# Reading P, q and k as rounded float32 in the TensorE transposes of a fused attention and gated-convolution kernel, with q and k in chunks of 128 and a work order planned by repeated passes

## The chip, the cores and the metric

The kernel runs on one core of one Trainium2 chip. The metric is the device time of one execution in microseconds (us). The kernel before takes 806.61 us, the median of three runs that lie between 805.94 and 806.62.

## The reference, cut to what matters

Eight batches, eight heads, 576 tokens, 64 values per head. Attention is causal by blocks of 64 tokens; its output, with the heads side by side, goes through a two-layer block with a three-tap convolution as a gate:

```python
scores = scale * np.matmul(q, k.transpose(0, 1, 3, 2))           # q, k, v: 8 x 8 x 576 x 64
scores = np.where(block_i >= block_j, scores, -1000000000.0)      # blocks of 64 tokens
scores = scores - np.max(scores, axis=-1, keepdims=True)
attn = np.exp(scores)
attn = attn / (np.sum(attn, axis=-1, keepdims=True) + 1e-09)
x = np.matmul(attn, v)                                            # -> 8 x 576 x 512
h = np.maximum(x @ w_in, 0.0)                                     # 512 -> 1024
conv_out[t] = sum(conv_w[k] * h[t + k - 1] for k in range(3))     # zero outside the sequence
out = (h / (1.0 + np.exp(-conv_out))) @ w_out                     # 1024 -> 512
```

## The kernel before, in words

**Numbers.** Nearly every product is made from operands that are split in two: a "high" part rounded to the format `float32r` (rounded float32; `F32R` in the code, `fp32r` or plain `f32` in the profile) and a "low" rest, also `float32r`. A product is then three TensorE passes: high by high, high by low, low by high. The names end in `h` and `l` (`qh`, `ql`, `ptbh`, `ptbl`, `xh`, `xl`, `wih`, `wil`, `woh`, `wol`, `gh`, `gl`).

**Tiling.** Heads go in pairs, 32 of them, four to a batch; a pair fills the 128 partitions with two times 64 values. The four pairs of the first batch are worked in two visits each ("A", the first 256 tokens, and "B", the rest), so that their part of the second stage can begin while weights are still loading; the other 28 pairs are one visit each.

For a pair of the 28:

- `load_nat` (L398) loads q and k with tokens on partitions into `qn` and `kn`: 6 pieces of 96 tokens, one DMA per head and tensor, from SyncE's queue (SP).
- `stage_t` (L707) turns them: for each of q and k two groups of three transposes (L725, 96x128 to 128x96) into one PSUM bank of the tag `w`, then ScalarE (ACT, L729) copies the high part and VectorE (DVE, L732) makes the low part, 288 tokens at a time. A transpose is a TensorE instruction in which the data are the stationary operand, loaded as weights, and the identity matrix `ident` is the moving one. DMAs from SP's queue then move high and low halves to other partitions (`qa`, `qb`, `ka`, `kb`, `qz`, `qdl`, L742 to L762).
- `stage_s` (L908) makes the scores of four blocks of 128 queries (L930, L932), their row maximum (DVE, L940) and the exponential P with its sum (ACT, L943), in tiles `p0` to `p3` of 128 to 512 keys. `last_s` (L872) does the last 64 queries of both heads together, in `p4` (576 keys). GpSimd (POOL) multiplies each P by the reciprocal of its sum (L859).
- `stage_x` (L1100) turns P: `one_bank` transposes 1 to 4 blocks of 128x128 into a bank of the tag `w` (L1116; 25 of them per pair), and ACT (L1126) and DVE (L1129) split the result into `ptah`/`ptal` or `ptbh`/`ptbl`.
- `stage_pv` (L1175) multiplies with v (L1203, L1207).

When four pairs of a batch are done, `ffn` runs the second stage in two halves of 288 tokens: the first layer (L1283), the gate on ACT, DVE and POOL, the second layer (L1342), the store. Its matmuls are small pieces of work that the order spreads among the attention of the next batch.

**The order.** Nothing is issued in the order of the code. Every piece of work is recorded by `Plan.op` with its engine, an assumed duration, the pieces that it depends on, the buffers that it uses and a target time. `Plan.order` (L97) then plays the program once on five assumed engines: each engine takes, of the pieces that are ready, the one with the lowest target. Second-stage matmuls are "paced": they may run at most `WINDOW` us ahead of the earliest attention piece that is still waiting. Where TensorE would idle for more than 0.4 us, `order` puts fill matmuls in (L1473), which compute nothing that is used. The result is one fixed order per engine. For a transpose group the plan assumes 0.109 us per P transpose and 0.084 us per q or k transpose.

Of the kernel before, what the change touches and what calls it, by code (L numbers as in the profile page):

```python
# [23 lines left out]
class Buf:  # L24


    def __init__(self, pool, shape, dtype, tag):
        self.args = (pool, shape, dtype, tag)
        self.uses = []
        self.before = []  # L30
        self.t = None

    @property
    def ap(self):
        if self.t is None:
            pool, shape, dtype, tag = self.args
            self.t = pool.tile(shape, dtype, tag=tag, name=tag)
        return self.t


# [13 lines left out]
class Plan:  # L54
# [41 lines left out]

    def order(self, window, skip, fill, clock):  # L97
        work, tags, unit, least, spare = fill
# [23 lines left out]
        for o in self.ops:  # L122
            o.left = len(o.deps)
            for d in o.deps:
                d.outs.append(o)
# [108 lines left out]
def kernel(  # L234
# [10 lines left out]
    nc = tc.nc  # L245
# [8 lines left out]
    HS = S // 2  # L254
    R = 6
    TP = S // R
    SCALE = 1.0 / 8.0
# [51 lines left out]
    WL0, WLS = -49.08, 2.41  # L309
    WINDOW = 19.66  # L310

    cp = ctx.enter_context(tc.tile_pool(name="cp", bufs=1))
# [14 lines left out]
    def one(shape, dtype, tag):  # L327
        return pl.buf(cp, shape, dtype, tag, 1)
# [26 lines left out]
    def two(shape, dtype, tag):  # L355
        return pl.buf(p2, shape, dtype, tag, 2)


    def c_mm(n, m=P):
        return max(n * 0.000447 + 0.005, 0.086 * m / P)  # L360

    def c_act(n, psum=True, ap=False, acc=False):
# [8 lines left out]
    def c_dma(n, packet):  # L371
        return n / (213e3 if packet < 512 else 290e3 if packet < 1024 else 330e3 if packet < 2048 else 390e3)
# [23 lines left out]


    def load_nat(p, at, part=None):  # L398
        b, h0 = p // NP, 2 * (p % NP)
        res = []  # L400
        for src, tag in ((q, "qn"), (k, "kn")):
            n = one([TP, R, 2, D], F32, tag)
            tok, w, r_ = (slice(Q1, S), 80, 4) if part else (slice(0, S), TP, R)

            def go(src=src, n=n, tok=tok, w=w, r_=r_):
                for j in range(2):
                    nc.sync.dma_start(out=n.ap[0:w, 0:r_, j, :],
                                      in_=src[b, h0 + j, tok, :].rearrange("(r p) d -> p r d", r=r_))

            res.append((n, pl.op(SP, 1.0, go, at, bufs=[n], xfer=2 * c_dma(r_ * w * D * 4, 256))))  # L410
        return res
# [295 lines left out]
    def stage_t(nat, at):  # L707
# [5 lines left out]
        for which, (n, ld) in enumerate(nat):  # L713
# [3 lines left out]
            es = []  # L717
            for j in range(2):
                tb = bank("tv")
                nn = HS  # L720
                tok = slice(HS * j, HS * j + HS)

                def tr(n=n, tb=tb, j=j):
                    for r in range(3):
                        nc.tensor.transpose(tb.ap[:, r * TP:(r + 1) * TP],  # L725
                                            n.ap[0:TP, 3 * j + r].rearrange("p j d -> p (j d)"), ident[0:TP, 0:TP])
# [74 lines left out]
    def rest_t(nat, at):  # L801
# [4 lines left out]
        for which, (n, ld) in enumerate(nat):  # L806
            hi, lo = (t["qa"], t["qb"]) if which == 0 else (t["kh"], t["kl"])
            scale = SCALE if which == 0 else 1.0
            w, rs, c0 = 80, ((0, 4),), Q1
            for j, (r0, r1) in enumerate(rs):  # L810
                tb = bank("tv")
                nn = w * (r1 - r0)
                tok = slice(c0 + w * r0, c0 + w * r1)

                def tr(n=n, tb=tb, r0=r0, r1=r1, w=w):
                    for r in range(r0, r1):
                        nc.tensor.transpose(tb.ap[:, (r - r0) * w:(r - r0 + 1) * w],
                                            n.ap[0:w, r].rearrange("p j d -> p (j d)"), ident[0:w, 0:w])
# [9 lines left out]
                o = pl.op(PE, (r1 - r0) * (w / 1200.0 + 0.004), tr, t0, deps=[ld], bufs=[n, tb], area=0.36)  # L828
# [43 lines left out]
    def last_s(t, ready4, t0, pb, done, exps, part):  # L872
        st4 = keep([P, 16], F32, "st4", 2, EPS)
        p4 = one([P, S], F32, "p4")
        pb[4] = p4
# [32 lines left out]
    def stage_s(ops, hh, at, part, shared):  # L908
# [52 lines left out]
    def stage_sb(ops, at):  # L961
# [4 lines left out]
        for z, i in enumerate((2, 3)):  # L966
# [18 lines left out]
            for hh in range(2):  # L985
                pt = two([P, nk], F32, f"p{i}")
                pb[hh][i] = pt
# [33 lines left out]
    def stage_sa(ops, at):  # L1021
# [3 lines left out]
        sb = [bank("s"), bank("f")]  # L1025
        pb = [{i: two([P, 128 * (i + 1)], F32, f"p{i}") for i in range(2)} for _ in range(2)]
        done, exps = [{}, {}], []
# [72 lines left out]
    def stage_x(pbd, hh, at, part, shared):  # L1100
# [10 lines left out]
        def one_bank(trs, rows, n, hi, lo, deps, t0, bufs_p, bufs_hi, bufs_lo, sub_ok, tag, shape):  # L1111
            tb = bank(tag)

            def tr():
                for z, (x, c, kk, col) in enumerate(trs):
                    nc.tensor.matmul(tb.ap[0:kk, col:col + P], pb[x].ap[:, 128 * c:128 * c + kk], ident,  # L1116
                                     start=(z == 0), stop=True, is_transpose=True, skip_group_check=True)

            o = pl.op(PE, len(trs) * 0.109 + 0.003, tr, t0, deps=deps, bufs=[tb] + bufs_p, area=0.49)

# [389 lines left out]
```

## Time and profile before

| what | value |
|---|---|
| runs | 806.61 us (805.94 to 806.62) |
| profiled execution, its own span from first to last instruction | 805.2 us |
| TensorE (PE) busy, 5381 matmuls | 793.4 us, 99% |
| VectorE (DVE) busy | 649.9 us, 81% |
| ScalarE (ACT) busy | 614.6 us, 76% |
| GpSimd (POOL) busy | 424.1 us, 53% |
| P transposes, L1116 | 800, of which 32 are 64 wide |
| q and k transposes of the 28 pairs, L725 | 336 |
| q and k transposes of visit "B", L817 | 32 |
| fill matmuls, L1473 | 100, all before 96 us |

The span is the only time that belongs to the profiled execution itself; the median of the runs is 1.4 us above it.

How to read the profile: a line such as `L1116 PE MATMUL w<-ident,p` is an operation of line 1116 on TensorE that writes a tile of the tag `w` from the moving operand `ident` and the stationary operand `p`. `PEld` is the load of the stationary operand, which can run beside the matmul before it. Matmuls are pipelined: the "mean" of one is how long it was in the engine, not how far apart two of them start. The distance from start to start is what TensorE spends on one; it is read from the timeline and from the chain of work.

### The profile page before, as it was taken

The page shows a single profiled execution, that of the slowest core. Times are in us where ns is not written, and L with a number is a line of the kernel's source. Part 1 is how long each engine was busy: PE and PEld are TensorE (multiplying, and loading weights), DVE is VectorE, ACT ScalarE, POOL GpSimd, SP SyncE. Part 2 cuts the span into 40 slices and gives each one's busy share as a digit, 9 for nine tenths or more (in the row PEclk, how much of TensorE's full clock was granted, in tenths as well). Part 3 has the DMA queues.
Part 4 walks back from the last instruction along what each step waited for, and adds up shares of the span by engine and source line. Part 5 has one row for each costly group of instructions (what it writes and reads, how often), then busy time and mean ns, then how long its engine had stood idle before and what let it go on. Part 6 is the DMA issues. An engine that isn't in the chain of part 4 may idle for free.

```text
span 805.2 us, 17261 instructions
## 1 busy us (share of the span) xinstructions
PE 793.4 (99%) x5381; PEld 712.1 (88%) x5381; DVE 649.9 (81%) x1889; ACT 614.6 (76%) x1769; POOL 424.1 (53%) x607
## 2 busy tenths in 40 slices
PE   8999999999999999999999999999999999999998
PEld 5668889888989899898989889898989989899996
DVE  6898989988979779797988869798887959887541
ACT  4769978977968769796978769697877858787652
POOL 3345556666655446565555645555455635546431
PEclk9999999999999999999999999999999999999999
DMA  9423556475445545444455544445554434540001
GB/s 231 143 65 92 144 122 149 111 182 145 104 116 125 134 118 120 110 101 120 120 135 135 122 117 99 102 115 135 135 122 118 110 98 105 136 105 14 14 27 40
DMA packets 163327, 91.35 MB, mean 113 GB/s; under 512 B 134540, under 2 KB 138660, under 8 KB 163236
## 3 DMA queue, kind: packets, MB, share of 16 engines
q1 hardware_dynamic: 162692, 90.12, 45.1%
q8 instruction: 44, 0.72, 0.4%
q14 instruction: 47, 0.39, 0.2%
q10 hardware_dynamic: 544, 0.13, 0.1%
HBM read 38.30 MB, written 9.44 MB: 59 GB/s over the span
## 4 chain that ended last, share of the span: by engine, by line
PE 82%; ACT 6%; DVE 5%; DMA 2%; issue 2%; POOL 2%; SPq 1%; ACTq 0%; POOLq 0%; DVEq 0%
PE f L1283 21%; PE f L1342 19%; PE w L1207 10%; PE w L1116 9%; PE s L930 4%; PE s L932 4%; PE w L1342 3%; PE s L885 3%; PE w L725 3%; PE s L1283 2%; ACT ptbh L1126 1%; DMA vn<-in_v_dram 1%; POOL vv L437 1%; DMA gh<-in_moe_w_in_dram 1%; PE s L1473 1%
## 5 line engine op out<-in xcount | busy, mean ns | idle before, releaser
L859 POOL TENSOR_SCALAR p<-p,st 128x256 f32<-128x256 f32 (+4 forms) x256 | 140.4, 562 | 139.0 <-DVE st L853 82.8
L1323 POOL TENSOR_TENSOR gl<-t,gh 128x288 fp32r<-128x288 f32 (+2 forms) x128 | 104.1, 816 | 148.8 <-ACT gh L1320 145.4
L943 ACT ACTIVATE p<-s,st 128x128 f32<-128x128 f32 x224 | 118.0, 527 | 41.9 <-DVE st L940 40.8
L1116 PE MATMUL w<-ident,p 128*128 128x128 f32 (+1 forms) x800 | 125.0, 274 | 0.7 <-DVE xl L1231 0.3
L940 DVE TENSOR_REDUCE st<-s 128x1 f32<-128x128 f32 x224 | 107.5, 484 | 3.4
L1126 ACT ACTIVATE ptbh<-w 128x384 fp32r<-128x384 f32 (+1 forms) x192 | 93.7, 508 | 21.7 <-PE w L1116 19.2
L1116 PEld LDWEIGHTS w<-ident,p 128*128 128x128 f32 (+1 forms) x800 | 95.0, 139 | 15.5 <-POOL p L859 1.7
L1342 PE MATMUL f<-woh,gh 128*128 128x512 f32 x248 | 103.9, 419 | 0.0
L1283 PE MATMUL f<-xh,wih 128*128 128x290 f32 (+2 forms) x480 | 97.7, 307 | 0.3 <-DVE t L1316 0.3
L1342 PE MATMUL f<-woh,gl 128*128 128x512 f32 x248 | 97.9, 395 | 0.0
L1129 DVE TENSOR_TENSOR ptbl<-w,ptbh 128x512 fp32r<-128x512 f32 (+1 forms) x144 | 89.6, 633 | 10.3 <-ACT ptbh L1126 7.4
L1342 PE MATMUL f<-wol,gh 128*128 128x512 f32 x248 | 97.7, 394 | 0.0
L1283 PE MATMUL f<-xh,wil 128*128 128x290 f32 (+2 forms) x480 | 94.5, 304 | 0.0
L1283 PE MATMUL f<-xl,wih 128*128 128x290 f32 (+2 forms) x480 | 93.3, 304 | 0.0
L1304 DVE SCALAR_TENSOR_TENSOR t<-f,cw,t 128x287 f32<-128x287 f32 (+3 forms) x120 | 59.9, 499 | 19.0 <-ACT t L1300 17.3
L1283 PEld LDWEIGHTS f<-xh,wih 128*128 128x128 f32 x480 | 73.1, 189 | 1.9 <-DVE t L1316 0.5
L1283 PEld LDWEIGHTS f<-xl,wih 128*128 128x128 f32 x480 | 72.9, 189 | 1.0
L1283 PEld LDWEIGHTS f<-xh,wil 128*128 128x128 f32 x480 | 73.2, 189 | 0.4
L932 PE MATMUL s<-kl,qz 128*128 128x128 f32 x224 | 72.1, 322 | 0.0
L1320 ACT ACTIVATE gh<-t 128x288 fp32r<-128x288 f32 (+2 forms) x128 | 56.7, 445 | 8.3 <-DVE t L1316 7.4
L1300 ACT ACTIVATE t<-f,cw 128x288 f32<-128x288 f32 (+2 forms) x120 | 59.9, 499 | 3.8
L1308 DVE SCALAR_TENSOR_TENSOR t<-f,cw,t 128x288 f32<-128x288 f32 (+3 forms) x120 | 60.6, 505 | 1.3
(230 smaller groups left out, 2001.0 us busy)
## 6 DMA issues: line engine op xcount, KB each, us to landing
out_dram<-stage SPq DMA_DIRECT2D x36, 256.0 KB, 2.2
vn<-in_v_dram SPq DMA_DIRECT2D x64, 128.0 KB, 2.9
qn<-in_q_dram SPq DMA_DIRECT2D x56, 144.0 KB, 2.9
kn<-in_k_dram SPq DMA_DIRECT2D x56, 144.0 KB, 3.1
ka<-kh SPq DMA_DIRECT2D x56, 144.0 KB, 2.6
kb<-kh SPq DMA_DIRECT2D x56, 144.0 KB, 2.6
qa<-qh SPq DMA_DIRECT2D x28, 144.0 KB, 2.4
qb<-qh SPq DMA_DIRECT2D x28, 144.0 KB, 2.6
```

The lines of the kernel that those rows point to most:

```text
L859: nc.gpsimd.tensor_scalar(out=pt.ap, in0=pt.ap, scalar1=st.ap[:, col:col + 1], scalar2=0.0, op0=ALU.mult, op1=ALU.add)
L932: nc.tensor.matmul(sb.ap[:, 0:nk], qz.ap[:, z:z + 128], kl.ap[:, 0:nk], start=False, stop=True)
L940: nc.vector.tensor_reduce(out=st.ap[:, i:i + 1], in_=sb.ap[:, 0:nk], op=ALU.max, axis=AX.X, negate=True)
L943: nc.scalar.activation(out=pt.ap[:, 0:nk], in_=sb.ap[:, 0:nk], func=AF.Exp, bias=st.ap[:, i:i + 1], accum_out=st.ap[:, 4 + 2 * i:5 + 2 * i])
L1116: nc.tensor.matmul(tb.ap[0:kk, col:col + P], pb[x].ap[:, 128 * c:128 * c + kk], ident, start=(z == 0), stop=True, is_transpose=True, skip_ ...
L1126: nc.scalar.activation(out=hi(), in_=src(), func=AF.Copy)
L1129: nc.vector.tensor_tensor(out=lo(), in0=src(), in1=hi(), op=ALU.subtract)
L1207: nc.tensor.matmul(tb.ap[0:m, q0 - qa:qb - qa], vv.ap[:, chunk(c), hh, w[ps_]], pm.ap[:, 128 * c + q0:128 * c + qb] if qa == 0 else pm.ap[ ...
L1283: nc.tensor.matmul(fb.ap[:, 0:n2], wt[:, c, fs], xs[c][xi].ap[:, x0:x0 + n2], start=(n + c - c0 == 0), stop=(n + c - c0 == 3 * NCC - 1))
L1308: nc.vector.scalar_tensor_tensor(out=t.ap[:, 0:i1], in0=fb.ap[:, own + 1:own + 1 + i1], scalar=cw[:, 2 * NFC + f:2 * NFC + f + 1], in1=t.a ...
L1323: nc.gpsimd.tensor_tensor(out=gbuf[1].ap[:, f, carry:carry + no], in0=t.ap[:, 0:no], in1=gbuf[0].ap[:, f, carry:carry + no], op=ALU.subtract)
L1342: nc.tensor.matmul(fb.ap[:, 0:DM], gbuf[a].ap[:, f, cs], w[:, f, :], start=(f == 0 and n == 0), stop=(f == NFC - 1 and n == 2))
```

## The change

1. **A second name for the same bytes.** The tiles `p0` to `p4`, `qn` and `kn` no longer come from tile pools. They lie at fixed addresses, each under two names: a float32 one, which ACT, POOL and the DMAs write, and a `float32r` one (`raw`, named `p3r`, `qnr` and so on), which only the transposes read. The numbers of buffers stay: two of each `p0` to `p3`, one of `p4`, `qn`, `kn`.
2. **All P, q and k transposes use `rident`**, the identity in `float32r`, and write PSUM through a `float32r` view. The transposes of the first 256 tokens of the first batch (L784) stay as they were.
3. **q and k in chunks of 128 tokens**: four chunks of 128 and one of 64 where there were six of 96 (in visit "B" two of 128 and one of 64 where there were four of 80). The two groups per tensor become three chunks (384 tokens) and two (192), where both were 288. Each load is three DMAs where it was two.
4. **The order by passes.** `order` now calls the forward play (`forward`, the old code) 25 times. After each, `late` plays the program backward from its end and gives every piece, as its new target, the latest time at which it could run; `WINDOW` is lifted after the first round. The order with the earliest planned end is kept.
5. **Assumed durations**: a group of n transposes counts as max(0.083 n - 0.035, 0.06) us.

```diff
+class Twin(Buf):
+    def __init__(self, pair):
+        self.t, self.raw = pair
...
+    def late(self, done):
...
+                if not left[d.seq]:
+                    heapq.heappush(future[d.eng], (rt[d.seq], top - d.end, d.seq, d))
+        return [top - r for r in res]
+
+    def order(self, window, skip, fill, clock, rounds):
+        best, least = None, 1e30
+        for _ in range(rounds + 1):
+            done = self.forward(window, skip, fill, clock)
+            end = max(o.end for o in self.ops)
+            if end < least:
+                best, least = done, end
+            for o, t in zip(self.ops, self.late(done)):
+                o.target = t
+            window = 1e9
+        return best
+
+    def forward(self, window, skip, fill, clock):
...
+    spans = [(f"p{i}", 128 * (i + 1), 2) for i in range(4)] + [("p4", S, 1), ("qn", 5 * P, 1), ("kn", 5 * P, 1)]
...
+            twins[tag].append([nc.alloc_sbuf_tensor_at(f"{tag}{x}{i}", [P, n], d, offset=at).ap()
+                               for x, d in (("f", F32), ("r", F32R))])
...
+    def c_tr(n):
+        return max(n * 0.083 - 0.035, 0.06)
...
+    def chunks(n, tb, cs):
+        for z, c in enumerate(cs):
+            m = P if c < 4 else 64
+            nc.tensor.transpose(tb.ap[:, P * z:P * z + m].bitcast(F32R), n.raw[0:m, P * c:P * c + P], rident[0:m, 0:m])
...
-            n = one([TP, R, 2, D], F32, tag)
+            n = twin(tag)
...
                 for j in range(2):
-                    nc.sync.dma_start(out=n.ap[0:w, 0:r_, j, :],
-                                      in_=src[b, h0 + j, tok, :].rearrange("(r p) d -> p r d", r=r_))
+                    nc.sync.dma_start(out=x[:, c0:4, j, :],
+                                      in_=src[b, h0 + j, P * c0:4 * P, :].rearrange("(c p) d -> p c d", p=P))
+                nc.sync.dma_start(out=x[0:64, 4, :, :], in_=src[b, h0:h0 + 2, 4 * P:S, :].rearrange("j p d -> p j d"))
...
-            for j in range(2):
+            for j, cs in enumerate(((0, 1, 2), (3, 4))):
                 tb = bank("tv")
-                nn = HS
-                tok = slice(HS * j, HS * j + HS)
+                nn = (384, 192)[j]
+                tok = slice(384 * j, 384 * j + nn)
...
-                o = pl.op(PE, 3 * (TP / 1200.0 + 0.004), tr, t0 + 0.5 * j, deps=[ld], bufs=[n, tb], area=0.36)
+                o = pl.op(PE, c_tr(len(cs)), tr, t0 + 0.5 * j, deps=[ld], bufs=[n, tb], area=0.7)
...
-            pt = two([P, nk], F32, f"p{i}")
+            pt = twin(f"p{i}")
...
-                    nc.tensor.matmul(tb.ap[0:kk, col:col + P], pb[x].ap[:, 128 * c:128 * c + kk], ident,
+                    nc.tensor.matmul(tb.ap[0:kk, col:col + P].bitcast(F32R), pb[x].raw[:, 128 * c:128 * c + kk], rident,
                                      start=(z == 0), stop=True, is_transpose=True, skip_group_check=True)
 
-            o = pl.op(PE, len(trs) * 0.109 + 0.003, tr, t0, deps=deps, bufs=[tb] + bufs_p, area=0.49)
+            o = pl.op(PE, c_tr(len(trs)), tr, t0, deps=deps, bufs=[tb] + bufs_p, area=0.8)
...
-    for o in pl.order(WINDOW, SKIP, (work, NBANK, 0.234, LEAST, SPARE), CLOCK):
+    for o in pl.order(WINDOW, SKIP, (work, NBANK, 0.234, LEAST, SPARE), CLOCK, ROUNDS):
```

The change moves work on every engine, because the plan is made anew. Two places are shown, on the two engines that the change touches itself. Rows are an engine's instructions in issue order; what is in brackets are the engines or DMA queues that an instruction waits for.

First TensorE, in the middle of the program, where the q and k transposes of the next pair stand among the scores and the second layer. Before (`kb`, `qb`, `kl`, `qz` are operands of the scores, `woh`, `gh` of the second layer, `p_` with a number is a P tile):

```order
L1342 MATMUL f<-woh,gl 128x512
L725 MATMUL w<-ident,qn 128x96 [waits PE_49]
L725 MATMUL w<-ident,qn 128x96 x2
L725 MATMUL w<-ident,qn 128x96 [waits DVE_49]
L725 MATMUL w<-ident,qn 128x96 x2
L930 MATMUL s<-kb,qb 128x256 [waits Activation_49]
L932 MATMUL s<-kl,qz_105 128x256
L1342 MATMUL f<-woh,gh 128x512
L1342 MATMUL f<-wol,gh 128x512
L1342 MATMUL f<-woh,gl 128x512
L725 MATMUL w<-ident,kn 128x96 [waits DMAHW7_49,DMAHW0_49,DVE_49]
L725 MATMUL w<-ident,kn 128x96 x2
```

The same place of the changed kernel (`qnr`, `knr` and `p0r` are the second names):

```order
L1024 MATMUL s<-kl,qz_127 128x256
L491 MATMUL w<-rident,qnr_95 128x128 [waits PE_49]
L491 MATMUL w<-rident,qnr_95 128x128 x2
L491 MATMUL w<-rident,qnr_95 128x128 [waits DVE_49]
L491 MATMUL w<-rident,qnr_95 128x64
L491 MATMUL w<-rident,knr_97 128x128 [waits DMAHW6_49,DMAHW7_49,DMAHW0_49,DVE_49]
L491 MATMUL w<-rident,knr_97 128x128 x2
L1022 MATMUL s<-kb,qb 128x384 [waits Activation_49]
L1024 MATMUL s<-kl,qz_127 128x384
```

Six transposes of q became five, the first group of k moved up to stand right behind them, ahead of a block of scores, and k now waits for three DMAs.

Then SyncE's queue at one pair, between two loads of k. Before:

```order
L407 DMA qn<-in_q_dram 96x6x64 x2
L762 DMA qa<-qh 64x576
L762 DMA qb<-qh 64x576
L742 DMA qz_105<-qh 64x576
L762 DMA qa<-ql 64x576
L762 DMA qb<-ql 64x576
L742 DMA qz_105<-qh 64x512
L762 DMA ka<-kh 64x576 x2
L762 DMA kb<-kh 64x576 x2
```

In the changed kernel:

```order
L503 DMA qnf_94<-in_q_dram 128x4x64 x2
L505 DMA qnf_94<-in_q_dram 64x2x64
L857 DMA qa<-qh 64x576
L837 DMA qz_127<-qh 64x576
L857 DMA qa<-ql 64x576
L837 DMA qz_127<-qh 64x512
L857 DMA ka<-kh 64x576 x2
L837 DMA qz_127<-qh 64x64
L846 DMA qdl_129<-ql 64x64 x2
L857 DMA qb<-qh 64x576
L857 DMA qb<-ql 64x576
L857 DMA kb<-kh 64x576 x2
```

The load of q is three issues ahead of the moves in place of two, and what the second head's scores need (`qb`, `kb`) now comes behind what the first head's need.

More of the change, by code (lines that the diff above doesn't have):

```diff
@@ L92, in op @@
         return o
-    def order(self, window, skip, fill, clock):
+    def late(self, done):
+        ops = self.ops
+        top = max(o.end for o in ops)
+        left = [len(o.outs) for o in ops]
+        rt = [0.0] * len(ops)
+        free, port = [0.0] * 5, 0.0
+        ready, future = [[] for _ in range(5)], [[] for _ in range(5)]
+        for o in ops:
+            if not left[o.seq]:
+                heapq.heappush(future[o.eng], (0.0, top - o.end, o.seq, o))
+        n = len(ops)
+        res = [0.0] * n
+        while n:
+            best = None
+            for e in range(5):
+                t = free[e]
+                while future[e] and future[e][0][0] <= t:
+                    o = heapq.heappop(future[e])[3]
+                    heapq.heappush(ready[e], (top - o.end, o.seq, o))
+                if ready[e]:
+                    p, _, o = ready[e][0]
+                    cand = (max(t, port) if o.port else t, p, e, o, 0)
+                elif future[e]:
+                    t, p, _, o = future[e][0]
+                    cand = (max(t, port) if o.port else t, p, e, o, 1)
+                else:
+                    continue
+                if best is None or cand[:2] < best[:2]:
+                    best = cand
+            t, _, e, o, where = best
+            heapq.heappop(future[e] if where else ready[e])
+            end = t + (o.end - o.start)
+            free[e] = end
+            if o.port:
+                port = end
+            res[o.seq] = end
+            n -= 1
+            for d in o.deps:
+                lat = self.DRAIN[d.eng] + (self.SIGNAL[e] if d.eng != e else 0.0) if (d.eng != PE or e != PE) else 0.0
+                rt[d.seq] = max(rt[d.seq], end + d.lat + lat)
+                left[d.seq] -= 1
+                if not left[d.seq]:
+                    heapq.heappush(future[d.eng], (rt[d.seq], top - d.end, d.seq, d))
+        return [top - r for r in res]
@@ L717, in stage_t, with tr @@
             es = []
[L718 removed]
+            for j, cs in enumerate(((0, 1, 2), (3, 4))):
                 tb = bank("tv")
[L720 to L726 removed]
+                nn = (384, 192)[j]
+                tok = slice(384 * j, 384 * j + nn)
+                def tr(n=n, tb=tb, cs=cs):
+                    chunks(n, tb, cs)
                 def ev_hi(tb=tb, hi=hi, scale=scale, tok=tok, nn=nn):
@@ L808, in rest_t, with tr @@
             scale = SCALE if which == 0 else 1.0
-            w, rs, c0 = 80, ((0, 4),), Q1
-            for j, (r0, r1) in enumerate(rs):
+            for j in range(1):
                 tb = bank("tv")
[L812 to L818, printed above, removed]
+                nn = S - Q1
+                tok = slice(Q1, S)
+                def tr(n=n, tb=tb):
+                    chunks(n, tb, (2, 3, 4))
                 def ev_hi(tb=tb, hi=hi, scale=scale, tok=tok, nn=nn):
```

37 lines of the change are left out of this document (28 added, 9 removed).

## The prediction, made before the changed kernel was run

> **What bounds the kernel now.** I read the page first, then busy time by stretch, then who waited for whom, then the chain of work in the middle, and last the timeline there. The page:
>
> ```profile
> span 805.2 us, 17261 instructions
> PE 793.4 (99%) x5381; PEld 712.1 (88%) x5381; DVE 649.9 (81%) x1889; ACT 614.6 (76%) x1769; POOL 424.1 (53%) x607
> PEclk9999999999999999999999999999999999999999
> PE f L1283 21%; PE f L1342 19%; PE w L1207 10%; PE w L1116 9%; PE s L930 4%; PE s L932 4%; PE w L1342 3%; PE s L885 3%; PE w L725 3%; PE s L1283 2%; ACT ptbh L1126 1%; DMA vn<-in_v_dram 1%; POOL vv L437 1%; DMA gh<-in_moe_w_in_dram 1%; PE s L1473 1%
> ```
>
> TensorE is busy 99% of the span at the full clock, and the chain that ended last runs over it, with 9% in the P transposes (L1116) and 3% in those of q and k (L725). A busy TensorE can still be a waiting one, so the stretches (us from:to, length, busy time and instructions of PE, PEld, DVE, ACT and POOL, clock, DMA share, GB/s) and TensorE's waits between 100 and 740 us come next:
>
> ```profile
> 80.00:100.00 20.00, 19.81 (x146) 16.15 (x145) 19.52 (x59) 19.32 (x53) 10.17 (x16) 1.00 0.54 148
> 100.00:740.00 640.00, 637.61 (x4419) 584.80 (x4420) 542.67 (x1602) 508.51 (x1484) 359.62 (x501) 1.00 0.49 119
> 740.00:801.00 61.00, 61.00 (x351) 54.33 (x350) 23.75 (x51) 29.50 (x73) 17.94 (x23) 1.00 0.07 27
> ...
> PE s L930 <- DMA ka<-kh: 1.1, 1, 1.1
> PE f L606 <- DVE wol L553: 0.4, 1, 0.4
> PE f L1283 <- DVE t L1316: 0.3, 1, 0.3
> PE s L930 <- ACT p L943: 0.2, 1, 0.2
> ```
>
> From 100 to 740 us TensorE waited 2.0 us in all, while DVE worked 542.67 of 640 us, 85%. From 740 us on there is only the second layer's stage of the last batch, and TensorE fills all of it. So TensorE's own work sets the end, and what is taken from it after 100 us should come off the span, as long as no other engine takes its place. Before 100 us this is not so: in the stretch from 80 to 100 us DVE was busy for 19.52 us of 20.
>
> **What a transpose costs.** Start-to-start distances come from the chain of work (start, duration, line, count), for P, for q, for the small ones of visit "B" and, last, for six ordinary matmuls of 512 columns:
>
> ```profile
> 406.80 0.77 PE w L1116 x7
> ...
> 424.47 0.50 PE w L725 x6
> ...
> 47.16 0.28 PE w L817 x4
> ...
> 408.70 1.40 PE f L1342 x6
> ```
>
> A P transpose takes 0.77/7 = 0.110 us, one of 96 columns 0.50/6 = 0.083, one of 80 columns 0.28/4 = 0.070, an ordinary matmul 1.40/6 = 0.233. The transposes scale with the columns of the moving identity, some 0.00086 us each, twice the 0.233/512 = 0.00046 of an ordinary matmul. All three load 128 columns of stationary data, so that load, read as float32 in a transpose, fits into 0.070 us.
>
> In rounded float32 the trace has only ordinary matmuls. From the timeline, two score matmuls of 128 columns between long ones; and the mean duration of weight loads of four kinds:
>
> ```profile
> 423.38 0.22 PE L930 MATMUL s<-kb,qb 128*128 128x128 f32 x1
> 423.44 0.27 PE L932 MATMUL s<-kl,qz 128*128 128x128 f32 x1
> 423.55 0.45 PE L1342 MATMUL f<-woh,gh 128*128 128x512 f32 x1
> ...
> L1116 PEld LDWEIGHTS w<-ident,p 128*128 128x128 f32 (+1 forms) x800 | 95.0, 139 | 15.5 <-POOL p L859 1.7 <-POOL p L1072 1.0 <-DVE ptbl L1129 0.8
> L725 PEld LDWEIGHTS w<-ident,qn 96*128 96x128 f32 x168 | 18.4, 140 | 2.4 <-issue 0.2
> L932 PEld LDWEIGHTS s<-kl,qz 128*128 128x128 f32 x224 | 42.5, 190 | 2.0
> L1207 PEld LDWEIGHTS w<-ptbl,vv 128*64 128x64 f32 x256 | 26.8, 136 | 0.9
> ```
>
> The second of the two starts 0.06 us after the first, because its weights were loaded under the long matmul before. The third starts 0.11 us after the second: its load could begin only with the second matmul, and 128 columns of rounded float32 need that long. A load of 64 columns is 54 ns shorter (190 - 136), which fits 0.11 us for 128. The float32 load in a transpose takes 139 ns for 128 columns, like an ordinary one of 64.
>
> So a rounded transpose of 128 columns moves in 0.06 us, and the question is its load. No row shows a rounded load in the transposing form. **Bounds** for the distance L between two transposes of a run: 0.058 (the move, 128 x 0.00046, if the load is as short as the float32 one) and 0.110 (if it is like every other rounded load). The nearest rows are the loads of the same 4-byte words in the same form, L1116 and L725; the shortest distance at which such a load of 128 columns has been seen to go by is the 0.070 of L817. I take L = 0.070.
>
> **The sum.** In the printed order the change has 1104 transposes in 317 unbroken runs: 800 of P, 304 of q and k. The last of a run is followed by an ordinary load, so it costs 0.11 whatever L is. Before there are 800 of P, 336 and 32 of q and k, in 316 runs, 97 of which end on q or k and pay 0.025 more there (0.108 - 0.083).
>
> - Before: 800 x 0.110 + 336 x 0.083 + 32 x 0.070 + 97 x 0.025 = 88.0 + 27.9 + 2.2 + 2.4 = 120.5 us.
> - After: 787 x L + 317 x 0.11 = 55.1 + 34.9 = 90.0 us at L = 0.070, a saving of 30.5. At 0.058 it is 40.0, at the 0.083 of today's q and k 20.3, at 0.110 it is -0.9.
>
> How many of them stand where TensorE is the bound, by the P transposes alone in the two stretches:
>
> ```profile
> 0.00:100.00 100.00, 13.29 (x81) 9.08 (x81) 1.00 0.51 135
> 100.00:740.00 640.00, 111.69 (x719) 85.97 (x719) 1.00 0.49 119
> ```
>
> - 719 of 800 come after 100 us, nine tenths: **-27.4** (from -36.0 at 0.058 to -18.3 at 0.083).
>
> In the Trainium skill, page "TensorE: Matmul & The Clock Gate", section "Back-to-back issue gap", a stream of load and matmul pairs of 128 columns settles at about 81 ns each. As an estimate by that figure the term would be -19.7 and the time some 788 us; the 0.070 of L817 went by with loads of the same 128 columns, so here the row goes ahead of the rule, which stays inside the range.
>
> Other edits, term by term:
>
> - *Fill matmuls* go from 100 to 90, and from 87 to 67 ahead of the first matmul of the second stage. Ten times 0.233 is 2.3 us of planned idleness less, all before 100 us. But the stretch 80 to 100 us shows DVE and ACT full, and what frees there need not come off: **-1**, between 0 and -2.3.
> - *Evictions.* ACT and DVE still copy twice per tensor, 384 + 192 tokens in place of 288 + 288: the same instructions and elements, nothing.
> - *Buffers.* As many as before, at fixed places: the same waits for a free one, nothing. If a stall hides here, it would show as TensorE or ACT waiting for a P tile; there is none above 0.2 us now.
> - *Loads.* One more DMA per tensor on SP's queue, ahead of the moves that the scores need. The queue at a pair (start, duration):
>
> ```profile
> 402.29 0.86 SPq L407 DMA_DIRECT2D qn<-in_q_dram  x2
> ...
> 405.85 0.55 SPq L762 DMA_DIRECT2D qa<-qh  x1
> 406.50 0.54 SPq L762 DMA_DIRECT2D qa<-ql  x1
> ...
> 414.18 1.08 SPq L407 DMA_DIRECT2D kn<-in_k_dram  x2
> 417.11 0.37 SPq L1355 DMA_DIRECT2D out_dram<-stage  x1
> ```
>
> An issue takes 0.86/2 = 0.43 us. The moves at this pair are issued from 405.85 to 414.18, and scores (L930) waited for one in only one place (1.1 us, above), so the cover is the second-stage matmuls that stand between q's transposes and the next scores: nothing now, 0.43 us per tensor if that cover went.
>
> *New waits.* With 27 us less, DVE's 542.67 us fall into 613 us, 89%, and every chain ACT - DVE - POOL has 4% less time under TensorE. The new order holds no fill after the first stage, so it leaves no planned gap of 0.4 us. But it is one order in fixed queues, and the row of 80 to 100 us shows that DVE can reach 98%. I put **+2**, between 0 and +7.
>
> 805.2 - 27.4 - 1 + 2 = 778.8 us of span, and 1.4 us more for the median of the runs (806.6 against a span of 805.2): **780.2 us**. The ends: 805.2 - 36.0 - 2.3 + 1.4 = 768.3 and 805.2 - 18.3 + 7 + 1.4 = 795.3.
>
> **The rivals.**
>
> *The load stays long.* If rounded weights load in a transpose as they do everywhere else in this trace, L is 0.110. P gains nothing, and five chunks of q cost more than six pieces of 96. That is -0.9 us of saving and a time of 805.2 + 0.9 + 1.4 = 807.5, no change. The same holds if the move of the rounded identity keeps the 0.00086 us per column of today. In its favour: every rounded load of 128 columns takes some 190 ns. Against: the load does depend on the form, since a transpose's takes 139 ns for the same 128 columns and 140 with 96 rows. Break-even is at (120.5 - 34.9)/787 = 0.109. Chance 0.09.
>
> The Trainium skill's rule for a load, in "LDWEIGHTS (loading the stationary operand)" of the same page, is columns divided by 1.2 GHz, 107 ns for 128, whatever the rows. By it, as an estimate, nine tenths of 1.4 us would go and this rival is right, at some 805 us; the trace agrees for rounded loads (0.11 us) and contradicts it for float32 ones in transposes (at most 0.070).
>
> *The moves come late.* The place is SP's queue between the load of q and the moves `qa`, `ka`, `qz`. One issue more ahead of them delays the scores by 0.43 us or more, twice a pair, and TensorE waits in order. With 28 pairs and a full 0.6 us (a move's issue takes 0.55, the next starts 0.65 later) at both tensors that is 33.6 us: 778.8 + 33.6 + 1.4 = 813.8, slower. It decides where the unhidden delay passes 27.4/56 = 0.49 us per tensor. For it: `qb` and `kb` come later in the new queue. Against: one DMA wait in 640 us, and SP issues nothing between 414.18 + 1.08 and 417.11 us in the pair shown. Chance 0.03.
>
> *The bound moves to the chain behind TensorE.* DVE at 89% on average has stretches at 98%; if waits of 15 us come back, the time is 795. For it: TensorE has never run against DVE at over 85% for long. Against: 2.0 us of waits in 640. Chance 0.10.
>
> **How the numbers follow.** The forecast's own case, L between 0.058 and 0.09 with TensorE still the bound, has 0.78. The range takes its two ends, 768 to 796, and leaves out the load rival, the late moves and the tails. A measurement of this kernel can tell about 0.2%, 1.6 us. Faster: 0.78 + 0.10 + a rest of the load rival where L is just under 0.109 and the start gains (0.02) = 0.90. Same: 0.06 of that rival. Slower: its last 0.01 and the late moves' 0.03 = 0.04.
>
> **What would show it.** In the changed profile: the chain should give a P transpose (L1208) about 0.07 us each inside a run; their weight loads about 140 ns, not 190; TensorE's busy time near 763 us; DVE's and ACT's busy time unchanged; TensorE's waits between 100 us and the end of attention under 7 us; the last stretch after attention still 61 us. Loads at 190 ns, or transposes 0.11 apart, prove the first rival. `L1022 <- DMA` high in TensorE's waits proves the second. TensorE waiting for DVE or ACT by more than 10 us proves the third.

## The result and the profile after

The changed kernel takes 801.62 us, the median of four runs (800.50 to 802.71), against 806.62 for the kernel before (four runs, 805.94 to 806.99): a ratio of 0.994 (0.9925 to 0.9954). It is faster by 5.0 us, clear of the noise but under 1%, where 26.4 were forecast, and lies above the range. The profiled execution has a span of 798.7 us and a time of 800.50.

The page after has TensorE as the bound, as before, and ACT's and DVE's work nearly as it was:

```profile
span 798.7 us, 17165 instructions
PE 784.3 (98%) x5307; PEld 698.8 (87%) x5307; DVE 642.2 (80%) x1889; ACT 617.8 (77%) x1769; POOL 427.4 (54%) x607
PEclk9899999999999999999999999999999999999999
PE f L1375 25%; PE f L1434 22%; PE w L1299 12%; PE w L1208 7%; PE s L1022 5%; PE s L1024 4%; PE w L491 4%; PE w L1434 4%; PE s L977 3%; PE s L1375 2%; PE s L1068 1%; DMA gh<-in_moe_w_in_dram 1%; PE s L1565 0%; PE w L1224 0%; POOL p0f L1164 0%
```

In the chain that ended last the P transposes fell from 9% to 7% (L1208), but those of q and k rose from 3% to 4% (L491), although there are fewer of them. And one slice near the start shows a clock under 0.9, which the kernel before does not have.

By stretches (columns as in the prediction's table), and TensorE's waits from 100 to 740 us:

```profile
100.00:740.00 640.00, 638.03 (x4412) 579.03 (x4411) 537.42 (x1610) 513.83 (x1491) 360.20 (x502) 1.00 0.51 120
...
732.00:793.00 61.00, 61.00 (x353) 54.38 (x352) 24.43 (x53) 30.25 (x74) 18.99 (x24) 1.00 0.07 27
```

```profile
PE s L1022 <- DMA ka<-kh: 0.7, 1, 0.7
PE w L1299 <- DVE ptbl L1221: 0.6, 1, 0.6
PE s L1022 <- ACT p1f L1035: 0.3, 1, 0.3
```

TensorE sits idle for 2.0 us of 640 (2.4 before), and waits for one move from SP's queue (0.7 us). The last stretch is still 61 us. So the missing 21 us aren't waits for another engine: TensorE does its own work more slowly than forecast. The weight loads, in groups, look just as forecast:

```profile
L1208 PEld LDWEIGHTS w<-rident,p3r 128*128 128x128 f32 x256 | 28.0, 141 | 3.0 <-issue 0.2
...
L491 PEld LDWEIGHTS w<-rident,qnr 128*128 128x128 f32 (+1 forms) x152 | 18.4, 140 | 5.5 <-issue 2.9
```

140 ns, not 190. What does not fit is the last column of the second row: the loads of q were idle before for 5.5 us, 2.9 of them for no cause that the profile shows. The loads at one pair (start, duration) show where:

```profile
423.47 0.14 PEld L491 LDWEIGHTS w<-rident,qnr 128*128 128x128 f32 x1
423.85 0.14 PEld L491 LDWEIGHTS w<-rident,qnr 64*128 64x128 f32 x1 [0.24 <-issue]
424.03 0.19 PEld L1022 LDWEIGHTS s<-kb,qb 128*128 128x128 f32 x1
424.14 0.19 PEld L1024 LDWEIGHTS s<-kl,qz 128*128 128x128 f32 x1
```

and the matmuls there:

```profile
423.47 0.39 PE L1434 MATMUL f<-woh,gl 128*128 128x512 f32 x1
423.70 0.40 PE L491 MATMUL w<-rident,qnr 128*128 128x128 f32 x2
424.03 0.39 PE L1022 MATMUL s<-kb,qb 128*128 128x256 f32 x1
```

The load of the first chunk runs under the long matmul. The next chunk has 64 tokens, so 64 rows of the array, and its load is not pulled ahead: it starts at 423.85, 0.15 us after the transpose before it started. The 128-row load behind it comes 0.18 us later still. From the first transpose of the two to the next score it is 0.33 us; twice L would be 0.14.

### The profile page after: what moved, and what is told of

Read it like the earlier page. It is cut to its first block, busy times and chain, and to the rows that moved or that the text cites. A ratio compares the mean times of both kernels' runs of the same rounds, so it can differ in the third digit from the quotient of the medians.

```text
span 798.7 us, 17165 instructions
## 1 busy us (share of the span) xinstructions
PE 784.3 (98%) x5307; PEld 698.8 (87%) x5307; DVE 642.2 (80%) x1889; ACT 617.8 (77%) x1769; POOL 427.4 (54%) x607
## 4 chain that ended last, share of the span: by engine, by line
PE 91%; DVE 4%; ACT 2%; POOL 1%; DMA 1%; issue 1%; SPq 0%; ACTq 0%; POOLq 0%; DVEq 0%
PE f L1375 25%; PE f L1434 22%; PE w L1299 12%; PE w L1208 7%; PE s L1022 5%; PE s L1024 4%; PE w L491 4%; PE w L1434 4%; PE s L977 3%; PE s L1375 2%; PE s L1068 1%; DMA gh<-in_moe_w_in_dram 1%; PE s L1565 0%; PE w L1224 0%; POOL p0f L1164 0%
## 5 line engine op out<-in xcount | busy, mean ns | idle before, releaser
L1415 POOL TENSOR_TENSOR gl<-t,gh 128x288 fp32r<-128x288 f32 (+2 forms) x128 | 103.5, 812 | 148.6 <-ACT gh L1412 131.2
L1218 ACT ACTIVATE ptbh<-w 128x384 fp32r<-128x384 f32 (+2 forms) x192 | 94.5, 508 | 16.7 <-PE w L1208 15.5
L1375 PE MATMUL f<-xh,wih 128*128 128x290 f32 (+2 forms) x480 | 95.5, 307 | 0.3 <-ACT p1f L1149 0.3
L951 POOL TENSOR_SCALAR p0f<-p0f,st 128x128 f32<-128x128 f32 x56 | 20.9, 373 | 121.4 <-DVE st L945 82.7
L1313 ACT ACTIVATE xt<-w 64x256 f32<-64x256 f32 x112 | 44.7, 402 | 29.4 <-PE w L1299 27.5
L1316 DVE TENSOR_TENSOR xt<-w,xt 64x256 f32<-64x256 f32 x112 | 51.4, 460 | 16.7 <-ACT xt L1313 13.4
L1405 ACT ACTIVATE t<-t 128x288 f32<-128x288 f32 (+2 forms) x128 | 56.4, 442 | 5.9 <-DVE t L1400 5.3
```

Source lines behind the costliest of these rows:

```text
L1218: nc.scalar.activation(out=hi(), in_=src(), func=AF.Copy)
L1375: nc.tensor.matmul(fb.ap[:, 0:n2], wt[:, c, fs], xs[c][xi].ap[:, x0:x0 + n2], start=(n + c - c0 == 0), stop=(n + c - c0 == 3 * NCC - 1))
L1405: nc.scalar.activation(out=t.ap[:, 0:no], in_=t.ap[:, 0:no], func=AF.Tanh)
L1415: nc.gpsimd.tensor_tensor(out=gbuf[1].ap[:, f, carry:carry + no], in0=t.ap[:, 0:no], in1=gbuf[0].ap[:, f, carry:carry + no], op=ALU.subtract)
```

## The experiments

Three theories stood for the missing time. The 64-row chunk: each switch between 64 and 128 rows makes loads and matmuls take turns. A longer L: rounded loads in transposes are farther apart than the 0.070 us of the float32 ones, for all rows. The order: the passes plan with costs that are wrong, and give time away somewhere. All medians below are of four runs, and the chains ran once; the kernel before had 806.16, 806.27 and 806.91 us on the three chips used.

### Full rows in the last chunk

```diff
+    for tag in ("qn", "kn"):
+        nc.gpsimd.memset(twins[tag][0][0][64:P, 4 * P:5 * P], 0.0)
...
-            m = P if c < 4 else 64
-            nc.tensor.transpose(tb.ap[:, P * z:P * z + m].bitcast(F32R), n.raw[0:m, P * c:P * c + P], rident[0:m, 0:m])
+            nc.tensor.transpose(tb.ap[:, P * z:P * z + P].bitcast(F32R), n.raw[:, P * c:P * c + P], rident)
```

> The changed kernel with its last chunk of q and k (tokens 512 to 575) transposed from all 128 partitions, of which 64 hold zeros that nobody reads, in place of 64. Theory A (rows): in the changed trace the load of a 64-row transpose starts only 0.15 us after the transpose before it, and the next 128-row load only 0.176 us after the 64-row transpose; against 0.083 and 0.108 in an unbroken run that is some 0.245 us for each of 64 such chunks with their reloads, 15.7 us, nine tenths of it on the path. A expects 787 us (785 to 791), the 128-row chunk at 0.085 like the others, and the transposes of q and k at some 22 us of TensorE's start-to-start time in place of 34.7. Theory B (order): the new order has taken the gain back by waits and by its start, and rows cost nothing; then the time stays at 800 to 803 us.

Measured: 786.80 us, ratio 0.9762 (0.9743 to 0.9782). Moving 128 columns where 64 are needed makes the kernel 14.8 us faster. There are 64 such chunks (32 pairs, q and k), so each stands for 0.23 us. At one pair the two chunks and what follows them:

```profile
417.67 0.29 PE L493 MATMUL w<-rident,knr 128*128 128x128 f32 x2
417.79 0.25 PE L1210 MATMUL w<-rident,p0r 128*128 128x128 f32 x1
```

0.12 us from the first chunk to the next transpose, where the change had 0.33. Where the same instruction follows, a first-layer matmul of 290 columns, the two chunks take 0.327 us in the changed kernel and 0.124 here (medians of 20 places in each trace): 0.20 us a chunk, 13.0 us for 64 of them. The 64-row theory holds, at the time that it expected, and it carries most of the error.

### The order alone

The kernel before with the passes; transposes, loads, buffers and assumed costs stay.

```diff
+    def late(self, done):
...
-    for o in pl.order(WINDOW, SKIP, (work, NBANK, 0.234, LEAST, SPARE), CLOCK):
+    for o in pl.order(WINDOW, SKIP, (work, NBANK, 0.234, LEAST, SPARE), CLOCK, 24):
```

> The kernel before with the 25 plays and nothing else: float32 transposes, chunks of 96, the durations that the plan assumed before. Theory A (rows): the order costs only where the changed trace is late, at the start (its second layer begins at 111.3 us, before at 106.0), and TensorE stays full afterwards; expected 805 to 810 us, with nothing lost after 110 us. Theory B (order): the order itself is worse throughout; expected 815 us or more. If the new order is better, below 804 us, it hid part of the loss.

Measured: 799.03 us, ratio 0.991 (0.989 to 0.993): the passes alone gain 7.1 us, the third case of the expectation. They hid part of the loss. TensorE's stretch from 110 to 740 us, of before and then with the passes:

```profile
110.00:740.00 630.00, 627.61 (x4349) 575.88 (x4348) 533.15 (x1577) 499.89 (x1459) 351.80 (x489) 1.00 0.49 118
```

```profile
110.00:740.00 630.00, 629.50 (x4379) 580.49 (x4378) 529.15 (x1577) 501.14 (x1459) 353.70 (x491) 1.00 0.49 118
```

1.9 us less idleness there, and 30 more matmuls in the same 630 us. The first stage is packed tighter too: the last fill matmul starts at 79.1 us (95.1 before), and the second layer begins at 103.5 us (106.0 before). These two make up 4.4 of the 7.1 us; the rest lies in TensorE's busy time, and no run shows where. The forecast had +1 us for the order.

### The changed kernel without the passes

```diff
-    ROUNDS = 24
+    ROUNDS = 0
```

> The changed kernel with the order of a single play and the old targets; the transposes are those of the change. Theory A (rows): the 64-row chunks are all there, so the loss after the start stays; expected 797 to 803 us, less than the change only by what its start costs (0 to 5 us). Theory B (order): without the new order the transposes pay in full; expected 780 to 790 us.

Measured: 811.94 us, ratio 1.0067 (1.005 to 1.0084). With one forward play, the changed transposes make the kernel slower by 5.8 us; neither theory expected that. All that the change gains hangs on the passes. A run below takes the 64-row chunk away under one play too.

### P rounded, q and k as before

The changed kernel with the old load, pieces of 96 and 80, and float32 transposes for q and k.

```diff
-            nc.tensor.transpose(tb.ap[:, P * z:P * z + m].bitcast(F32R), n.raw[0:m, P * c:P * c + P], rident[0:m, 0:m])
+                        nc.tensor.transpose(tb.ap[:, r * TP:(r + 1) * TP],
+                                            n.ap[0:TP, 3 * j + r].rearrange("p j d -> p (j d)"), ident[0:TP, 0:TP])
```

> The changed kernel with q and k loaded and transposed as before (float32, six pieces of 96, two DMAs); P's transposes rounded, the order by 25 plays. Theory A (rows): P saves 128 groups of three at 0.047 us and 96 of four at 0.071 us, 12.8 us, nine tenths on the path, and q and k cost what they did before; expected 794 to 798 us. Theory B (order): P's saving is taken back as well; expected 802 to 808 us.

Measured: 787.42 us, ratio 0.9761 (0.9742 to 0.978), below both ranges. P's part gains 11.6 us on top of the order. Turning q and k as the change does costs 14.2 (801.6 against 787.4), and with full rows gains 0.6 (786.8).

### Chains of one kind of transpose

Chains of 24 transposes or matmuls into one bank, each behind ordinary matmuls that keep the clock up. `xr` is rounded, `xf` float32; `rows` is the count of active rows.

```diff
+    def tr_r(t, rows):
+        nc.tensor.transpose(t[:, 0:rows].bitcast(F32R), xr[0:rows, :], rident[0:rows, 0:rows])
+    def tr_f(t, rows):
+        nc.tensor.transpose(t[:, 0:rows], xf[0:rows, :], ident[0:rows, 0:rows])
+    def mm_r(t, rows):
+        nc.tensor.matmul(t[:, 0:P], xr[0:rows, :], wide[0:rows, 0:P], start=True, stop=True)
```

> Not the reference's computation: chains of 24 TensorE instructions each, on constants, with ordinary 512-column matmuls between the chains so that the clock is full; the output is zeros. Start to start within a chain. Theory A (rows): only a load of 64 rows next to one of 128 rows has to wait; expected rounded transposes of 128 rows 0.085 us, float32 ones 0.109, ordinary rounded 128-column matmuls 0.108, rounded transposes with 96 rows 0.085 and alternating 128 and 96 rows 0.085, alternating 128 and 64 rows 0.16 on average, of 64 rows alone 0.085. If the wait came from the rounded form and not from the rows, the float32 alternation would cost no more than 0.085 on average, and the ordinary one 0.108. Theory L1 (what makes 0.085): a rounded load in a transpose is longer than a float32 one, then 80 rows with an 80-column move still take 0.085 where float32 takes 0.070. Theory L2: the load is the same and 0.085 comes from the short move; then the float32 one of 80 rows would be the exception and the rounded one of 80 rows goes below 0.070.

From its chain of work (start, duration, line, count), without the matmuls between. L44 is `tr_f`, L41 `tr_r`, L47 `mm_r`. In this order: float32 128 rows, rounded 128, ordinary 128, float32 80, rounded 80, 96 and 64; then alternating rows, rounded 128/64, float32 128/64, rounded 128/96, ordinary 128/64:

```profile
12.60 2.62 PE bank L44 x24
...
18.88 2.02 PE bank L41 x24
...
24.64 2.63 PE bank L47 x24
...
31.02 1.66 PE bank L44 x24
...
36.37 1.96 PE bank L41 x24
...
42.10 1.98 PE bank L41 x24
...
47.79 2.10 PE bank L41 x24
...
53.78 4.47 PE bank L41 x24
...
62.09 5.87 PE bank L44 x24
...
74.30 1.96 PE bank L41 x24
...
79.99 7.28 PE bank L47 x24
```

| chain | us each (duration/24) |
|---|---|
| float32, 128 rows / 80 rows | 0.109 / 0.069 |
| rounded, 128 / 96 / 80 / 64 rows | 0.084 / 0.083 / 0.082 / 0.088 |
| ordinary rounded matmul of 128 columns, 128 rows | 0.110 |
| rounded, alternating 128 and 96 rows | 0.082 |
| rounded, alternating 128 and 64 rows | 0.186 |
| float32, alternating 128 and 64 rows | 0.245, the end of it below full clock; 0.23 before that |
| ordinary rounded, alternating 128 and 64 rows | 0.303, part of it at half clock; 0.256 before that |

Two things follow. *The switch*: 64 rows alone cost hardly more than others (0.088), but alternating with 128 they take twice as long and more, in every form; the rounded pair was expected at 0.16 each and takes 0.186. 96 with 128 costs nothing. *The period*: the rounded transpose is 0.084 apart with 128 columns to move and still 0.082 with 80, so it isn't the move that sets it; float32 with 80 takes 0.069. And where the first load had been taken ahead, as before the two chunks at 417.67 in the kernel with full rows, the moves start 0.06 apart. So the load sets it, and a rounded load in a transpose is longer than a float32 one. Yet their records are equally long:

```profile
L41 PEld LDWEIGHTS bank<-rident,xr 128*128 128x128 f32 (+3 forms) x144 | 13.9, 139 | 2.4 <-issue 0.6
...
L44 PEld LDWEIGHTS bank<-ident,xf 128*128 128x128 f32 (+1 forms) x72 | 7.9, 141 | 2.9 <-issue 0.7
```

139 and 141 ns stand for periods of 0.084 and at most 0.069 us. The length of a load's record doesn't give the distance between two loads. In the changed kernel itself the period shows in the loads of a run: four P loads from 415.23, the next load at 415.57, 0.085 us each.

```profile
415.23 0.40 PEld L1208 LDWEIGHTS w<-rident,p3r 128*128 128x128 f32 x4
415.57 0.19 PEld L1022 LDWEIGHTS s<-ka,qa 128*128 128x128 f32 x1
```

Here the Trainium skill was nearer than the row that I took: "TensorE: Matmul & The Clock Gate", section "Back-to-back issue gap", has 81 ns for a pair of load and matmul at 128 columns, and the rounded transposes of 80 to 128 rows show 82 to 85; ordinary rounded matmuls of 128 columns, at 110, do not agree with it. Its section "LDWEIGHTS (loading the stationary operand)" says that rows don't matter to a load's time. That holds for chains of one height (0.082 to 0.088), and the record of the 64-row load at 423.85 is as long as the others (0.14 us); the wait where 64 and 128 alternate (0.186) comes on top of it.

### The plan told the true cost

Full rows, and the measured period in the assumed durations.

```diff
-        return max(n * 0.083 - 0.035, 0.06)
+        return n * 0.085 + 0.025
```

> The kernel with full 128-row chunks, and the plan told what a group of n transposes was measured to take: 0.085 n + 0.025 us in place of 0.083 n - 0.035. If the plan's wrong figure costs TensorE time (an order made for a faster TensorE leaves short gaps), 782 to 785 us; if the order is insensitive to it, 786 to 788 us.

Measured: 784.02 us, ratio 0.9722 (0.9705 to 0.9738), the fastest of all, 2.8 us under full rows alone. What it gains lies at the start, and the granted clock differs there (the last columns are clock, DMA share, GB/s). The changed kernel, then this one:

```profile
10.00:20.00 10.00, 6.48 (x32) 4.32 (x28) 9.46 (x28) 4.20 (x15) 5.85 (x5) 1.00 1.11 243
20.00:25.00 5.00, 4.93 (x22) 3.63 (x23) 1.49 (x6) 3.29 (x9) 4.17 (x9) 0.51 0.78 196
25.00:30.00 5.00, 5.00 (x28) 3.72 (x28) 3.83 (x11) 2.92 (x11) 0.47 (x2) 0.80 0.87 256
```

```profile
10.00:20.00 10.00, 9.54 (x49) 6.72 (x47) 9.68 (x30) 6.44 (x18) 5.09 (x7) 1.00 1.00 242
20.00:30.00 10.00, 9.64 (x62) 6.81 (x62) 9.05 (x24) 7.06 (x23) 6.74 (x12) 1.00 0.73 204
```

In the changed kernel TensorE is idle for 3.5 of 10 us before 20 us, two of its waits there being for GpSimd's P tiles,

```profile
PE w L1208 <- POOL p0f L1164: 1.5, 1, 1.5
PE w L1208 <- POOL p1f L1164: 1.4, 1, 1.4
```

and the clock is then granted at 0.51 and 0.80 for five us each: (0.49 + 0.20) x 5 = 3.4 us of TensorE's time, as an estimate. The runs of P alone say it is less: 785.87 us at a mean clock of 1.000 against 787.69 and 787.92 at 0.996, about 2 us. Full rows (0.70 from 20 to 30 us) and P alone (0.66) have the dip too; this kernel, the order alone and the kernel before have none. The second layer's first and last matmul, of the order alone, the changed kernel, full rows and this one:

```profile
L1401 PE MATMUL f<-woh,gh x248: 389/397/485, 103.5 to 738.7; 128*128 128x512 f32 x124
```

```profile
L1434 PE MATMUL f<-woh,gh x248: 389/397/506, 111.3 to 740.6; 128*128 128x512 f32 x124
```

```profile
L1436 PE MATMUL f<-woh,gh x248: 389/397/505, 108.7 to 726.8; 128*128 128x512 f32 x124
```

```profile
L1436 PE MATMUL f<-woh,gh x248: 389/397/497, 104.7 to 724.0; 128*128 128x512 f32 x124
```

The changed kernel starts that layer 7.8 us later than the order alone; this one only 1.2. Against full rows it starts the layer 4.0 us earlier and ends it 2.8 us earlier. From 110 to 740 us TensorE is idle for 1.8 us in both, so the gain is not in the short gaps that the expectation named. How much of it is the clock and how much the new order of the start, no run separates.

### The first fill from a zeroed tile

In the changed kernel the fills of the first microseconds read `rident`, and TensorE waits for that tile from DVE (1.6 us). The first fill is written to read a tile of zeros that is there earlier, but the list by which the code tells the first one is no longer empty after the first play. This edit, on full rows, clears the list at each play.

```diff
+        work(None, 0)
...
+        if b is None:
+            fills.clear()
+            return None
```

> The kernel with full 128-row chunks, and its first fill matmuls reading the zeroed tile again, as before the change, so that TensorE starts at 1.05 us and not at 1.62. Theory S1: the dip of the granted clock between 20 and 30 us (0.51 and 0.80 in the changed kernel) comes from TensorE's idle time between 10 and 20 us, which this does not touch; then 786 to 787 us and the dip stays. Theory S2: the dip comes from the late first matmuls; then the clock is 1.00 and the time 783 to 785 us.

Measured: 787.87 us, ratio 0.977 (0.9755 to 0.9784), no gain over 786.80. TensorE starts at 1.06 us, but the dip stays, so that first wait isn't its cause:

```profile
20.00:30.00 10.00, 9.91 (x46) 7.37 (x47) 4.94 (x16) 5.84 (x18) 4.26 (x10) 0.61 0.77 213
```

### True cost and first fill together

The two edits above in one kernel.

> The two edits before together: full chunks, measured cost in the plan, first fills from the zeroed tile. Expected the better of the two, 782 to 786 us; if the start's dip goes with the other order, below 783 us.

Measured: 784.60 us, ratio 0.9736 (0.9717 to 0.9755). Nothing on top of the true cost. The clock is full from 20 us on but was granted at 0.93 in the first ten us and at 0.90 in the next: this order has a dip too, only earlier.

### Full rows without the passes

The first edit, with `ROUNDS = 0`.

> The kernel with full 128-row chunks and the order of a single play. If the 64-row chunks cost the same under either order, it lies as far below the change with one play (811.9 us) as the full chunks lie below the change (14.8 us): 796 to 799 us, and the transposes alone, without the new order, are then worth 7 to 10 us against before. If the new order is what makes the faster transposes pay, 800 to 804 us.

Measured: 802.56 us, ratio 0.9942 (0.9925 to 0.9958), in the second of the two ranges: the new order is what makes the faster transposes pay. With full rows the passes are worth some 15 us (786.8 against 802.6), twice what they are worth to the old transposes. TensorE's stretch from 110 to 740 us, and its waits there:

```profile
110.00:740.00 630.00, 622.55 (x4342) 566.85 (x4341) 531.43 (x1590) 505.56 (x1472) 357.51 (x496) 1.00 0.49 119
```

```profile
PE s L1024 <- ACT p0f L1037: 1.4, 3, 0.7
PE s L1024 <- issue: 1.3, 3, 0.6
PE f L1377 <- DVE t L1410: 1.1, 4, 0.3
```

TensorE idles for 7.5 us, where it idled 2.4 before and 1.8 with the passes (628.19 of 630 busy with full rows). The waits are many small ones, for ACT and DVE. The 64-row chunk costs 9.4 us here (811.94 against 802.56, on two chips), less than under the passes: where TensorE waits anyway, part of it is hidden, though no run shows which part.

## Why the prediction was wrong, and where it was right

The mechanism that it named is there: rounded transposes are nearer to each other, TensorE stays the bound, and the gain comes off the span. The step that failed is the one under "The sum" that priced all 1104 transposes alike, "787 x L + 317 x 0.11". The listing of the new order in the section on the change shows the fourth chunk as `128x64`; the prediction noted that 96 rows load in as long a record as 128, and never asked what 64 rows among 128 cost. The code held a hint: in both kernels the plan adds 0.2 us, the last number of `CLOCK`, wherever a TensorE piece marked `rows64` follows one without the mark, or the other way round. Only the scores of the first batch's visits are marked; the new 64-row transposes are not, so the plan left their price out as the forecast did.

| step | forecast, us | the runs, us | error, us |
|---|---|---|---|
| the 64-row chunk costs what others cost | 0 | +14.8 (801.6 against 786.8) | +14.8 |
| L = 0.070 | -27.4 | -16.8 at the measured 0.085: 0.9 x (30.5 - 787 x 0.015) | +10.6 |
| fills -1, new waits +2 | +1 | -7.1, the order alone | -8.1 |
| full clock throughout | 0 | +3.4, estimated from the granted clock | +3.4 |
| sum | | | +20.7 of 21.4 |

The terms lean on each other (the passes are worth 7.1 us with the old transposes and some 15 with the new), and the last of them, the clock, is an estimate on the high side. So the table is one way to share the error out, and that its sum comes so near is partly luck.

- **L.** The bounds 0.058 and 0.110 held. The choice between them failed: L817's 0.070 was for float32 words, and a rounded load, with a record just as long, takes 0.085. The range's low end of the saving, at 0.083, was nearly right. The kernel with the true cost tests the term whole: 784.0 against 799.0 for the order alone is -15.0, near the -16.8 and far from -27.4. Both have the passes; without them, the new transposes with full rows gain 4.4 (802.56 against 806.91).
- **The order.** Priced as a risk only, because TensorE waited for just 2.0 us from 100 to 740 us. But the passes had gains elsewhere (a start 2.5 us earlier), and without them the faster transposes would have brought back waits.
- **The start.** "-1, between 0 and -2.3" has the wrong sign: the second layer begins 5.3 us later than before (111.3 against 106.0). The dip of the clock is part of that. That it comes from TensorE's idle microseconds right before it is only argued, and in two of the chains the clock fell while TensorE's records leave no gap; what in the order makes the dip, no run here isolates.
- **The rivals.** *The load stays long* is refuted: 140 ns records, 0.085 and not 0.110. It came near in its time for another reason. *The moves come late*: one wait of 0.7 us. *The bound moves to the chain behind TensorE*: not in the changed kernel (2.0 us), but it is what happens without the passes (7.5 us).
- **What held**: records of 140 ns (which don't tell the period, as the chains show), the cover over the third DMA, ACT and DVE with the same instructions (617.8 and 642.2 us busy), waits under 7 us, 61 us at the end. TensorE's busy time was to be near 763 us and is 784.3: that one line told that the time went into TensorE's own work.

## What to carry to other kernels

Where TensorE is the bound, count the active rows of every instruction in the row of work, not only its columns: a 64-row transpose between 128-row instructions cost 0.20 us, and padding the 64 of them with zeros to 128 rows won 14.8 us. If a planner comes with the kernel, look for the prices that it already holds. Take the price of an instruction from the distance between starts in a chain of its own kind and format, not from how long its record is. When an order is planned from assumed costs, measure those costs and give the plan the true ones; the one run that did so alone gained 2.8 us. Of the two kernels and their variants, the one with full rows and true costs is the fastest (784.0 us, 2.8% under before).

## What the runs showed of the hardware

- A load of 64 rows behind a 128-row transpose starts 0.15 us after that transpose started, and the next 128-row load 0.18 us later, in place of 0.085 each. Alternating 128/64 costs 0.186 us an instruction in rounded transposes and 0.23 in float32 ones at full clock; 128/96 costs nothing (0.082).
- In chains, transposes of rounded data are 0.082 to 0.088 us apart for 64 to 128 rows and columns; those of float32 0.069 at 80 and 0.109 at 128.
- Weight loads with records of 139 and 141 ns follow each other at 0.084 and 0.069 us.
- After 3.5 idle us in 10, the granted clock fell to 0.51 for about five us and was at 0.80 in the next five. The kernel with the true cost idled for 2.7 of its first 10 us and kept 1.00.
- The clock also fell without a gap in TensorE's records: after some four us of alternating 128/64 float32 transposes it was 0.70 from 66 to 67 us and 0.50 up to the end of the chain at 67.95; in the chain of alternating ordinary matmuls it was 0.50 from 84 us on.
